# The last matrix product of a fused attention and two-MLP kernel, made of seven block products instead of eight

## The chip, the cores and the metric

The kernel runs on one core of a Trainium2 chip. The metric is the device time of one execution in microseconds (us). The core's engines are TensorE (PE in the views; PEld is its weight load), VectorE (DVE), ScalarE (ACT), GpSimd (POOL) and SyncE (SP), which issues the DMAs. Each takes its instructions in order.

## The reference

```python
attn_out = _attn_ref(q, k, v)                  # 8 batches, 8 heads, 576 tokens, head size 64; k, v pooled by 8
x = attn_out.transpose(0, 2, 1, 3).reshape(B * S, H * D)      # 4608 x 512
x = _moe_ref(x=x, w_in, w_out, g_ln)           # SoLU MLP: softmax, layer norm, 512 -> 1024 -> 512
# second MLP:
a = x @ w1                                     # 4608 x 1024
b = x @ w2
h = a * b @ w3                                 # w3: 1024 x 1024
return (h @ w_out).astype(np.float32)          # w_out: 1024 x 512; called w_out2 in the kernel
```

## The kernel before

The program runs attention and the first MLP interleaved, then the second MLP, in float32. A matrix operand is kept as a rounded half and the rest (helper `split`: ScalarE rounds into the half `hi`, VectorE subtracts into `lo`), and a product is the sum of three matmuls, hi x hi, hi x lo and lo x hi. The second MLP is bilinear before w3, so (a * b) @ w3 @ w_out2 is computed as (a * b) times the 1024 x 512 matrix WF = w3 w_out2.

The 4608 tokens are nine units of 512 (`NB`; eight are one batch's first 512 tokens, the last collects the left-over 64 of each batch). Around the change the program is written out by hand for all five engines, so that each engine's order is that of the code:

1. `ab` makes a * b, transposed, in seven products a pair of blocks, and spills it to DRAM (`pd[j, fc]`: unit j, rows 128 fc to 128 fc + 127 of the 1024, 512 tokens).
2. WF is made in eight blocks of 128 rows. For each, `load_w3` loads 128 rows of w3, `w3_T` transposes them on TensorE (two times four 128 x 128) and splits them out of PSUM, and `wf_rows` multiplies them by the split w_out2 (24 matmuls of 512 columns) and splits the result into an SBUF pair. The transposes of a row block stand ahead of the product of the block before it; two buffers of transposed rows alternate. The text calls these eight blocks rows 0 to 7.
3. The last product: for each unit and each of the eight fc, `product` loads 128 x 512 of `pd`, splits it three steps ahead, and twelve matmuls of 512 columns add to four PSUM banks (`accs`). After the eighth, `evac` scales the four results by a factor of the token (`kap`) and stores them.

PSUM has eight banks, given out in turn by `bank`.

Of the kernel before, what the change touches and what calls it, by code (L numbers as in the profile page):

```python
# [18 lines left out]
def attention_moe_kernel(  # L19
# [1038 lines left out]

    o2, w3raw = [], {}
# [27 lines left out]
    def o2_tiles():  # L1087
        nonlocal STG
        xqs.close()
        STG = ctx.enter_context(tc.tile_pool(name="stage", bufs=1, reuse_waits="tile"))  # L1090
        for f in range(5):
            o2.append(STG.tile([P, 2, 512], F32R, tag=f"o{f}", name=f"o{f}"))

# [3 lines left out]

    STG, o2raw = None, {}

# [11 lines left out]
    def load_w3(m, i):  # L1111
        w3raw[m, i] = staged("w3f", 2 * m + i)

    def w3_pair(m):
        t = TH[(spare, slots[6])[m % 2]].rearrange("p (t f n) -> p t f n", t=2, f=FC)
# [10 lines left out]
    def wf_pair(fc):  # L1126
        t = TH[slots[2 + fc // 2]][:, fc % 2 * 1024 : fc % 2 * 1024 + 1024]
        return t[:, 0:512], t[:, 512:1024]

    def wf_rows(m):  # L1130

        th, tl = w3_pair(m)
# [6 lines left out]
        split(*wf_pair(m), ow)  # L1139

    E = mybir.EngineType
    with tc.manual_schedule(engines={E.PE, E.SP, E.Activation, E.DVE, E.Pool}):
# [22 lines left out]
        for m in range(FC):  # L1165
            for i in range(2):
                if m + 2 < FC:
                    load_w3(m + 2, i)
            for i in range(2):
                if m + 1 < FC:  # L1170
                    w3_T(m + 1, i)
            wf_rows(m)
        products.close()
        sums.close()
        OB = ctx.enter_context(tc.tile_pool(name="out", bufs=1, side="right", reuse_waits="tile"))

        def product(j, fc):
            t, h, l = [
                OB.tile([P, 512], d, tag=n, name=f"{n}{j}_{fc}", bufs=b)
                for n, d, b in (("pt", F32, 8), ("ph", F32R, 4), ("pl", F32R, 4))  # L1180
            ]
            nc.sync.dma_start(t, pd[j, fc])
            nc.scalar.activation(h, t, AF.Copy)  # L1183
            nc.vector.tensor_tensor(l, t, h.bitcast(F32), ALU.subtract)  # L1184
            return h, l

        def evac(j, t, acc):
            ot = OB.tile([P, C], F32, tag="ot", name=f"ot{j}_{t}", bufs=8)
            k = kap[:, 4 * j + t : 4 * j + t + 1]
            if t % 2 == 0:  # L1190
                nc.vector.tensor_scalar(ot, acc, k, None, ALU.mult)
            else:
                nc.scalar.activation(ot, acc, AF.Copy, scale=k)
            if j == B:
# [51 lines left out]
```

## Time and profile before

| | |
|---|---|
| three runs | 1258.39, 1261.03, 1261.51 us, median 1261.03 |
| profiled execution | 1258.51 us, of which the span from first to last instruction is 1256.6 |
| TensorE busy | 1205.6 us (96%), 6794 matmuls |
| VectorE, ScalarE, GpSimd busy | 735.7 (59%), 500.9 (40%), 425.4 us (34%) |
| granted TensorE clock, mean | 0.995 |
| HBM | 99.62 MB read, 48.23 MB written |

Busy time of TensorE is that of matmuls that overlap one another, so 96% says that it hardly pauses. The granted clock is a share of 2.4 GHz; its other level is 0.5, 1.2 GHz. Times in the rows are microseconds from the start of the span, durations us or ns as marked. "Idle before" and the name behind an arrow are the pause of an engine and what ended it.

### The profile page before, as it was taken

Reading aid. Unit: us, or ns where it says so; the run is one execution under the profiler, and the core shown is the slowest. Engines: PE = TensorE matmul, PEld = TensorE weight load, DVE = VectorE, ACT = ScalarE, POOL = GpSimd, SP = SyncE. Lnnn points to the kernel's source line nnn. Section 1 sums busy time; section 2 is a strip of 40 time slices with the busy share of each in tenths; the row PEclk is TensorE's granted clock in tenths of the full one; section 3 lists DMA queues with packets and bytes.
Section 4 is the critical chain, followed back from the end, with each engine's and each line's share of the span. In section 5 each row is a group of like instructions: output and inputs, shape, how many; then the busy total and the mean of one; then the engine's idle time right before and its main releaser. Section 6 shows DMA issues by size and latency. Waiting matters only on the chain. (4 is left out here: it accounts for less than half of the span.)

```text
span 1256.6 us, 18917 instructions
## 1 busy us (share of the span) xinstructions
PE 1205.6 (96%) x6794; PEld 1039.5 (83%) x6794; DVE 735.7 (59%) x1296; ACT 500.9 (40%) x1385; POOL 425.4 (34%) x452
## 2 busy tenths in 40 slices
PE   7868999999999999999898999999999999999998
PEld 5658888899999899999798888888878787888886
DVE  5758776767676767546667656666565622333322
ACT  5544756565656565645522112121121122232222
POOL 3523444344434352200037467494662200000000
PEclk9988999999999999999999999999999999999999
DMA  9561535454445453122341443424412430442533
GB/s 233 112 159 56 143 98 140 106 135 117 124 104 143 109 143 81 59 69 74 114 156 43 134 159 114 141 92 148 159 68 92 142 135 26 144 158 101 188 114 109
DMA packets 148158, 149.11 MB, mean 119 GB/s; under 512 B 81504, under 2 KB 91744, under 8 KB 148064
## 3 DMA queue, kind: packets, MB, share of 16 engines
q1 hardware_dynamic: 148064, 147.90, 39.9%
q8 instruction: 54, 0.88, 0.3%
q14 instruction: 40, 0.33, 0.1%
HBM read 99.62 MB, written 48.23 MB: 118 GB/s over the span
## 5 line engine op out<-in xcount | busy, mean ns | idle before, releaser
L687 PE MATMUL x<-lnh,gwh 128*128 128x256 f32 x576 | 166.1, 288 | 0.0
L688 PE MATMUL x<-lnl,gwh 128*128 128x256 f32 x576 | 163.3, 283 | 0.0
L689 PE MATMUL x<-lnh,gwl 128*128 128x256 f32 x576 | 163.1, 283 | 0.0
L981 ACT ACTIVATE p<-p 128x512 f32<-128x512 f32 (+1 forms) x40 | 22.3, 556 | 268.9 <-PE p L979 227.6
L1184 DVE TENSOR_TENSOR pl<-pt,ph 128x512 fp32r<-128x512 f32 x72 | 49.4, 691 | 128.9 <-ACT ph L1183 112.0
L1212 PE MATMUL acc<-th,ph 128*128 128x512 f32 x288 | 114.0, 396 | 1.2 <-ACT ph L1183 1.2
L1214 PE MATMUL acc<-th,pl 128*128 128x512 f32 x288 | 114.0, 396 | 0.1
L1213 PE MATMUL acc<-th,ph 128*128 128x512 f32 x288 | 113.9, 395 | 0.0
L688 PEld LDWEIGHTS x<-lnl,gwh 128*128 128x128 f32 x576 | 110.3, 191 | 1.3 <-DVE lnl L677 0.4
L687 PEld LDWEIGHTS x<-lnh,gwh 128*128 128x128 f32 x576 | 110.3, 191 | 1.0 <-DVE lnl L677 0.2
L689 PEld LDWEIGHTS x<-lnh,gwl 128*128 128x128 f32 x576 | 110.2, 191 | 0.0
L515 ACT ACTIVATE ea<-sc,mx 128x72 f32<-128x72 f32 x320 | 98.2, 331 | 14.7 <-DVE mx L512 13.7
L630 PE MATMUL h<-winh,xh 128*128 128x512 f32 x288 | 97.6, 420 | 2.9 <-DVE e L645 2.9
L1183 ACT ACTIVATE ph<-pt 128x512 fp32r<-128x512 f32 x72 | 45.2, 632 | 122.2 <-PE acc L1213 86.9
L535 POOL TENSOR_TENSOR pr<-ea,sm 128x512 f32<-128x512 f32 x40 | 43.2, 1080 | 147.4 <-DVE sm L531 69.5
L630 PE MATMUL h<-winl,xh 128*128 128x512 f32 x288 | 89.7, 393 | 0.0
L630 PE MATMUL h<-winh,xl 128*128 128x512 f32 x288 | 89.3, 392 | 0.0
L993 POOL TENSOR_TENSOR a<-a,b 128x512 f32<-128x512 f32 (+1 forms) x40 | 51.8, 1296 | 90.6 <-issue 72.9
L185 POOL TENSOR_TENSOR cvb<-cvb,cvm 128x512 int32<-128x512 int32 x33 | 42.8, 1297 | 98.1 <-DVE cvb L179 62.6
L677 DVE TENSOR_TENSOR lnl<-lt,lnh 128x512 fp32r<-128x512 f32 x72 | 49.2, 687 | 40.6 <-ACT lnh L676 40.0
L515 ACT ACTIVATION_READ_ACCUMULATOR ea<-sc,mx 128x1 f32 x320 | 69.6, 218 | 0.0
L1212 PEld LDWEIGHTS acc<-th,ph 128*128 128x128 f32 x288 | 54.1, 188 | 14.7 <-ACT ph L1183 1.6
(228 smaller groups left out, 3164.2 us busy)
## 6 DMA issues: line engine op xcount, KB each, us to landing
pt<-pd SPq DMA_DIRECT2D x72, 256.0 KB
pd<-a SPq DMA_DIRECT2D x64, 256.0 KB
out_dram<-ot SPq DMA_DIRECT2D x36, 256.0 KB
x2d<-xo SPq DMA_DIRECT2D x35, 256.0 KB
f<-in_moe_w_dram SPq DMA_DIRECT2D x17, 512.0 KB
kv<-in_k_dram SPq DMA_DIRECT2D x32, 256.0 KB
kv<-in_v_dram SPq DMA_DIRECT2D x32, 256.0 KB
f<-in_moe_w_out_dram SPq DMA_DIRECT2D x16, 512.0 KB
```

The source lines that it names most:

```text
L515: nc.scalar.activation(e[0:n, x], half[a][:, h], AF.Exp, bias=mx[0:n, x : x + 1], scale=1.0, accum_out=sm[0:n, x : x + 1],)
L630: nc.tensor.matmul(self.ph[:, a], s_[:, c], w_[:, c, a * 512 : a * 512 + 512], start=first, stop=last)
L677: after(1, lambda: nc.vector.tensor_tensor(lo, src, hi.bitcast(F32), ALU.subtract), first=0)
L687: nc.tensor.matmul(o, gw[0][:, f, ws], self.th[:, f], start=(f == 0), stop=False)
L688: nc.tensor.matmul(o, gw[0][:, f, ws], self.tl[:, f], start=False, stop=False)
L689: nc.tensor.matmul(o, gw[1][:, f, ws], self.th[:, f], start=False, stop=(f == FC - 1))
L993: nc.gpsimd.tensor_tensor(a[:, 0], a[:, 0], b[:, 0], ALU.mult)
L1183: nc.scalar.activation(h, t, AF.Copy)
L1184: nc.vector.tensor_tensor(l, t, h.bitcast(F32), ALU.subtract)
L1212: nc.tensor.matmul(accs[t], ph[:, ts], wh, start=(fc == 0), stop=False)
L1213: nc.tensor.matmul(accs[t], ph[:, ts], wl, start=False, stop=False)
L1214: nc.tensor.matmul(accs[t], pl[:, ts], wh, start=False, stop=(fc == FC - 1))
```

## The change

The last product is written as a 2 x 2 block product in seven multiplications. For unit j the four blocks of the left matrix are x11, x21 (first 512 of the 1024, first and second 256 tokens), x12, x22; those of WF are its upper and lower half by left and right 256 columns. GpSimd forms four sums of left blocks (`Last.sum`), and each of the seven factors of 4 x 128 x 256 is split (`Last.split`, one instruction of 128 x 1024 on ScalarE and one on VectorE). The seven combinations of WF are formed while WF is made: its row blocks come in pairs, one of the upper and one of the lower half (`HALVES`), `upper` keeps the first in SBUF, and `lower` makes differences and splits six combinations. `Last.product` multiplies (24 matmuls of 256 columns), `Last.use` adds the products (VectorE out of PSUM), scales the finished rows in SBUF (ScalarE) and stores them. The factors of unit j + 1 are split during unit j, in the order of its products; the loads of unit j + 2 are issued at the start of unit j. Unit 0's own come in `early`, its last three at the start of its products. The odd buffer of transposed rows moves to another tile.

```diff
+    HALVES = (0, 4, 1, 5, 2, 6, 3, 7)
...
     def load_w3(m, i):
-        w3raw[m, i] = staged("w3f", 2 * m + i)
+        w3raw[m, i] = staged("w3f", 2 * HALVES[m] + i)
     def w3_pair(m):
-        t = TH[(spare, slots[6])[m % 2]].rearrange("p (t f n) -> p t f n", t=2, f=FC)
+        t = TH[(spare, slots[5])[m % 2]].rearrange("p (t f n) -> p t f n", t=2, f=FC)
         return t[:, 0], t[:, 1]
...
-    def wf_pair(fc):
-        t = TH[slots[2 + fc // 2]][:, fc % 2 * 1024 : fc % 2 * 1024 + 1024]
-        return t[:, 0:512], t[:, 512:1024]
-    def wf_rows(m):
-        th, tl = w3_pair(m)
+    def wf_rows(n):
+        m = HALVES[n]
+        th, tl = w3_pair(n)
         ow = bank(f"ow{m}")
         for f in range(FC):
             oh, ol = o2[f][:, 0], o2[f][:, 1]
             nc.tensor.matmul(ow, th[:, f], oh, start=(f == 0), stop=False)
             nc.tensor.matmul(ow, th[:, f], ol, start=False, stop=False)
             nc.tensor.matmul(ow, tl[:, f], oh, start=False, stop=(f == FC - 1))
-        split(*wf_pair(m), ow)
+        return ow
+    def combined(k, c):
+        if k < 4:
+            return [t[:, k, c * U : c * U + U] for t in wc]
+        t = TH[slots[k - 2]].rearrange("p (t c n) -> p t c n", t=2, c=4)
+        return t[:, 0, c], t[:, 1, c]
+    def small(name, bufs=1):
+        return RB.tile([P, U], F32, tag=name, name=name, bufs=bufs)
+    def upper(c, ow):
+        w1_ = RB.tile([P, 2, U], F32, tag="wf", name="wf", bufs=2)
+        nc.scalar.activation(w1_, ow.rearrange("p (h n) -> p h n", h=2), AF.Copy)
+        split(*combined(0, c), w1_[:, 0])
+        t1 = small("t1")
+        nc.gpsimd.tensor_tensor(t1, w1_[:, 1], w1_[:, 0], ALU.subtract)
+        return w1_[:, 1], t1
+    def lower(c, ow, w12, t1):
+        tt = nc.vector.tensor_tensor
+        w21, w22 = ow[:, 0:U], ow[:, U : 2 * U]
+        t2, t3, t4 = small("t2"), small("t3"), small("t4")
+        split(*combined(3, c), w21)
+        tt(t2, w22, t1, ALU.subtract)
+        split(*combined(1, c), t2)
+        split(*combined(2, c), t1)
+        tt(t3, w22, w12, ALU.subtract)
+        split(*combined(4, c), t3)
+        tt(t4, w21, t2, ALU.subtract)
+        split(*combined(5, c), t4)
+        split(*combined(6, c), w22)
+    FACTORS = ("x11", "s2", "s1", "x12", "s3", "x22", "s4")
+    free = list(range(10))
+    class Last:
+        def __init__(self, j):
+            self.j, self.x, self.place = j, {}, {}
+            self.order = range(7) if j else (0, 3, 1, 2, 4, 5, 6)
+        def load(self, k):
+            t = RB.tile([P, 4, 512], F32, tag="raw", name=f"raw{self.j}_{k}", bufs=4)
+            nc.sync.dma_start(t, pd[self.j, 4 * k : 4 * k + 4].rearrange("f p n -> p f n"))
+            for i in range(2):
+                self.x[f"x{i + 1}{k + 1}"] = t[:, :, i * U : i * U + U]
+        def sum(self, name):
+            x = self.x
+            a, b, op = dict(
+                s1=("x21", "x22", ALU.add),
+                s2=("s1", "x11", ALU.subtract),
+                s3=("x11", "x21", ALU.subtract),
+                s4=("x12", "s2", ALU.subtract),
+            )[name]
+            x[name] = RB.tile([P, 4, U], F32, tag="s", name=f"{name}_{self.j}", bufs=4)
+            nc.gpsimd.tensor_tensor(x[name], x[a], x[b], op)
+        def split(self, k):
+            n = self.place[k] = free.pop(0)
+            t = BK[n].rearrange("p (t c n) -> p t c n", t=2, c=4)
+            split(t[:, 0], t[:, 1], self.x[FACTORS[k]])
+            self.x[k] = t[:, 0], t[:, 1]
+        def product(self, n):
+            k = self.order[n]
+            h, l = self.x[k]
+            o = bank(f"o{k}_{self.j}").rearrange("p (t n) -> p t n", t=2)
+            for t in range(2):
+                ts = slice(t * P, t * P + P)
+                for c in range(4):
+                    wh, wl = combined(k, c)
+                    nc.tensor.matmul(o[:, t], h[:, c, ts], wh, start=(c == 0), stop=False)
+                    nc.tensor.matmul(o[:, t], h[:, c, ts], wl, start=False, stop=False)
+                    nc.tensor.matmul(o[:, t], l[:, c, ts], wh, start=False, stop=(c == 3))
+            free.append(self.place[k])
+            self.use(k, o)
+        def scale(self, t, src, dst, i):
+            n = 4 * self.j + 2 * i + t
+            nc.scalar.activation(dst, src, AF.Copy, scale=kap[:, n : n + 1])
+        def tile(self, name):
+            return OT.tile([P, 2, U], F32, tag=name, name=f"{name}_{self.j}")
+        def store(self, i, t=None):
+            if self.j == B:
+                to = out.rearrange("(b s) c -> s b c", s=S)[512:S, 4 * i + 2 * t : 4 * i + 2 * t + 2, :]
+                nc.sync.dma_start(to, self.rows[i][:, t])
+            else:
+                r0 = S * self.j + 2 * P * i
+                nc.sync.dma_start(out[r0 : r0 + 2 * P].rearrange("(t p) c -> p t c", p=P), self.rows[i])
+        def use(self, k, o):
+            tt = nc.vector.tensor_tensor
+            lo, hi = slice(0, U), slice(U, 2 * U)
+            if k == 0:
+                self.p1 = self.tile("p1")
+                self.rows = [
+                    OT.tile([P, 2, C], F32, tag="rows", name=f"rows{self.j}_{i}", bufs=4) for i in range(2)
+                ]
+                nc.scalar.activation(self.p1, o, AF.Copy)
+            elif k == 1:
+                self.u2 = self.tile("u2")
+                tt(self.u2, self.p1, o, ALU.add)
+            elif k == 2:
+                self.u4 = self.tile("u4")
+                tt(self.u4, self.u2, o, ALU.add)
+            elif k == 3:
+                r = self.rows[0]
+                tt(r[:, :, lo], self.p1, o, ALU.add)
+            elif k == 4:
+                self.u3 = self.tile("u3")
+                tt(self.u3, self.u2, o, ALU.add)
+                tt(self.rows[1][:, :, hi], self.u4, o, ALU.add)
+            else:
+                i, x, cs = (1, self.u3, lo) if k == 5 else (0, self.u4, hi)
+                r = self.rows[i]
+                if self.j < B:
+                    tt(r[:, :, cs], x, o, ALU.add)
+                for t in range(2):
+                    if self.j == B:
+                        tt(r[:, t, cs], x[:, t], o[:, t], ALU.add)
+                    self.scale(t, r[:, t], r[:, t], i)
+                    if self.j == B:
+                        self.store(i, t)
+                if self.j < B:
+                    self.store(i)
...
         products.close()
         sums.close()
-        OB = ctx.enter_context(tc.tile_pool(name="out", bufs=1, side="right", reuse_waits="tile"))
...
+        RB = ctx.enter_context(tc.tile_pool(name="last", bufs=1, side="right", reuse_waits="tile"))
+        BK = [RB.tile([P, 2048], F32R, tag=f"bk{i}", name=f"bk{i}") for i in range(6)]
+        BK += [TH[i] for i in (spare, slots[0], slots[1], slots[5])]
+        wc = weight_pair(wp, "w16", [P, 4, F], "wc")
+        last = [Last(j) for j in range(NB)]
+        z = last[0]
+        early = {
+            1: [(z.load, 0)],
+            2: [(z.load, 1)],
+            3: [(z.split, 0)],
+            4: [(z.sum, "s1"), (z.sum, "s2"), (z.split, 3), (last[1].load, 0)],
+            5: [(z.sum, "s3"), (z.sum, "s4"), (z.split, 1), (last[1].load, 1)],
+            7: [(z.split, 2), (last[1].sum, "s1")],
+        }
+        for n in range(FC):
+            for i in range(2):
+                if n + 2 < FC:
+                    load_w3(n + 2, i)
+            for i in range(2):
+                if n + 1 < FC:
+                    w3_T(n + 1, i)
+            ow = wf_rows(n)
+            if n % 2 == 0:
+                w12, t1 = upper(n // 2, ow)
             else:
+                lower(n // 2, ow, w12, t1)
+            for fn, *args in early.get(n, ()):
+                fn(*args)
+        stg.close()
+        OT = ctx.enter_context(tc.tile_pool(name="out", bufs=1, reuse_waits="tile"))
+        for j, un in enumerate(last):
+            n1_, n2_ = [last[i] if i < NB else None for i in (j + 1, j + 2)]
+            for n in range(7):
+                if n == 0 and n2_:
+                    n2_.load(0)
+                    n2_.load(1)
+                if n1_ and n in (0, 2, 4):
+                    n1_.sum(("s2", "s3", "s4")[n // 2])
+                if n == 6 and n2_:
+                    n2_.sum("s1")
+                if un is z and n < 3:
+                    z.split(4 + n)
+                if n1_:
+                    n1_.split(n1_.order[n])
+                un.product(n)
```

ScalarE between row 5 and row 7 of WF. In the names, `pw6` are the transposed rows of row 6, `ow` are products of rows (numbered by their place in WF), and `th0`, `th6`, `th7` the buffers of transposed rows; the text calls the splits of `pw7` row 7's. Before:

```order
L100 ACTIVATE th0_7258<-pw6_0_10429 128x512
L100 ACTIVATE th0_7258<-pw6_1_10436 128x512
L100 ACTIVATE th5_7263<-ow5_10443 128x512
L100 ACTIVATE th7_7307<-pw7_0_10470 128x512
L100 ACTIVATE th7_7307<-pw7_1_10477 128x512
```

After (`t1` to `t4` are differences of WF's blocks, `wch` holds the rounded combinations 0 to 3, `th3` to `th5` those of 4 to 6, `bk2` a split factor, `s2_0` a sum of unit 0):

```order
L100 ACTIVATE th0_7258<-pw6_0_10501 128x512
L100 ACTIVATE th0_7258<-pw6_1_10508 128x512
L100 ACTIVATE wch_10212<-ow6_10515 128x256
L100 ACTIVATE wch_10212<-t2_10540 128x256
L100 ACTIVATE wch_10212<-t1_10487 128x256
L100 ACTIVATE th3_7261<-t3_10541 128x256
L100 ACTIVATE th4_7262<-t4_10542 128x256
L100 ACTIVATE th5_7263<-ow6_10515 128x256
L100 ACTIVATE bk2_10208<-s2_0_10491 128x1024
L100 ACTIVATE th6_7264<-pw7_0_10566 128x512
L100 ACTIVATE th6_7264<-pw7_1_10573 128x512
```

Between the splits of row 6 and those of row 7 there was one rounding; now there are six, each but the first and last of a difference made by another engine, and one of 1024 columns.

VectorE in the last product, unit 3 before (`pl` is the rest of a split, `ot` a scaled result):

```order
L1184 TENSOR_TENSOR pl3_3_11044<-pt3_3_11042,ph3_3_11043 128x512
L1184 TENSOR_TENSOR pl3_4_11066<-pt3_4_11064,ph3_4_11065 128x512
L1184 TENSOR_TENSOR pl3_5_11084<-pt3_5_11082,ph3_5_11083 128x512
L1184 TENSOR_TENSOR pl3_6_11102<-pt3_6_11100,ph3_6_11101 128x512
L1184 TENSOR_TENSOR pl3_7_11120<-pt3_7_11118,ph3_7_11119 128x512
L1184 TENSOR_TENSOR pl4_0_11138<-pt4_0_11136,ph4_0_11137 128x512
L1184 TENSOR_TENSOR pl4_1_11156<-pt4_1_11154,ph4_1_11155 128x512
L1184 TENSOR_TENSOR pl4_2_11174<-pt4_2_11172,ph4_2_11173 128x512
L1191 TENSOR_SCALAR ot3_0_11181<-acc3_0_11048,kap_78 128x512
L1191 TENSOR_SCALAR ot3_2_11193<-acc3_2_11050,kap_78 128x512
```

VectorE during unit 2 after (`o1_2` to `o6_2` are unit 2's products, `bk` and `th` on the left split factors of unit 3; the factors 0 and 1 stand just ahead):

```order
L1245 TENSOR_TENSOR u2_2_11174<-p1_2_11143,o1_2_11149 128x512
L101 TENSOR_TENSOR bk3_10209<-s1_3_11077,bk3_10209 128x1024
L1248 TENSOR_TENSOR u4_2_11205<-u2_2_11174,o2_2_11180 128x512
L101 TENSOR_TENSOR bk4_10210<-raw3_1_10891,bk4_10210 128x1024
L1251 TENSOR_TENSOR rows2_0_11144<-p1_2_11143,o3_2_11209 128x2x256
L101 TENSOR_TENSOR th0_7258<-s3_3_11176,th0_7258 128x1024
L1254 TENSOR_TENSOR u3_2_11264<-u2_2_11174,o4_2_11239 128x512
L1255 TENSOR_TENSOR rows2_1_11145<-u4_2_11205,o4_2_11239 128x2x256
L101 TENSOR_TENSOR th2_7260<-raw3_1_10891,th2_7260 128x1024
L1260 TENSOR_TENSOR rows2_1_11145<-u3_2_11264,o5_2_11269 128x2x256
L101 TENSOR_TENSOR bk5_10211<-s4_3_11235,bk5_10211 128x1024
L1260 TENSOR_TENSOR rows2_0_11144<-u4_2_11205,o6_2_11302 128x2x256
```

Eight subtractions and two scalings have become seven subtractions of double width and seven additions that alternate with them.

ScalarE during unit 3 before (`ph` is the rounded half):

```order
L1193 ACTIVATE ot2_1_11027<-acc2_1_10889,kap_78 128x512
L1193 ACTIVATE ot2_3_11039<-acc2_3_10891,kap_78 128x512
L1183 ACTIVATE ph3_3_11043<-pt3_3_11042 128x512
L1183 ACTIVATE ph3_4_11065<-pt3_4_11064 128x512
L1183 ACTIVATE ph3_5_11083<-pt3_5_11082 128x512
L1183 ACTIVATE ph3_6_11101<-pt3_6_11100 128x512
L1183 ACTIVATE ph3_7_11119<-pt3_7_11118 128x512
```

ScalarE during unit 2 after, with the factors of unit 3:

```order
L100 ACTIVATE bk1_10207<-raw3_0_10889 128x1024
L1242 ACTIVATE p1_2_11143<-o0_2_11118 128x512
L100 ACTIVATE bk2_10208<-s2_3_11114 128x1024
L100 ACTIVATE bk3_10209<-s1_3_11077 128x1024
L100 ACTIVATE bk4_10210<-raw3_1_10891 128x1024
L100 ACTIVATE th0_7258<-s3_3_11176 128x1024
L100 ACTIVATE th2_7260<-raw3_1_10891 128x1024
L1221 ACTIVATE rows2_1_11145<-rows2_1_11145,kap_78 128x512 x2
L100 ACTIVATE bk5_10211<-s4_3_11235 128x1024
L1221 ACTIVATE rows2_0_11144<-rows2_0_11144,kap_78 128x512 x2
```

The scalings of finished rows now stand between the roundings of the last factors, and each pair waits for an addition.

## Rows read from the trace of the kernel before

**Rows 1.** Windows: stretch; busy us of each engine (instructions); clock; DMA share, GB/s.

```profile
997.40:1048.80 51.40, 50.13 (x243) 40.87 (x241) 13.99 (x22) 11.23 (x21) 2.33 (x2) 1.00 0.34 113
1048.80:1050.20 1.40, 0.22 (x1) 0.00 (x0) 0.52 (x1) 1.15 (x3) 0.00 (x0) 1.00 0.00 0
1050.20:1252.30 202.10, 202.01 (x864) 162.01 (x864) 62.06 (x91) 56.23 (x88) 0.00 (x0) 1.00 0.36 125
1252.30:1256.60 4.30, 0.12 (x1) 0.00 (x0) 0.21 (x1) 0.69 (x1) 0.00 (x0) 1.00 0.66 244
```

**Rows 2.** Chain that ended last, two pieces in w3 w_out2: start, us, what.

```profile
1011.36 0.87 PE pw L1121 x8
1017.73 0.87 PE pw L1121 x8
```

**Rows 3.** TensorE's timeline, two stretches: start, us, line, operation, out<-in.

```profile
608.77 0.28 PE L687 MATMUL x<-lnh,gwh 128*128 128x256 f32 x1
...
611.89 0.28 PE L689 MATMUL x<-lnh,gwl 128*128 128x256 f32 x1
...
654.94 0.28 PE L977 MATMUL p<-th,s2h 128*128 128x256 f32 x1
...
656.94 0.28 PE L979 MATMUL p<-th,w1l 128*128 128x256 f32 x1
```

**Rows 4.** Groups of instructions: line, form, count; busy us, mean ns; idle before.

```profile
L1212 PEld LDWEIGHTS acc<-th,ph 128*128 128x128 f32 x288 | 54.1, 188 | 14.7 <-ACT ph L1183 1.6
L1183 ACT ACTIVATE ph<-pt 128x512 fp32r<-128x512 f32 x72 | 45.2, 632 | 122.2 <-PE acc L1213 86.9 <-DMA pt<-pd 33.9 <-DVE pl L1184 0.7
L100 ACT ACTIVATE th<-pw 128x512 fp32r<-128x512 f32 x16 | 8.9, 598 | 5.5 <-PE pw L1121 5.4
L983 DVE TENSOR_TENSOR u<-p,p 128x256 f32<-128x256 f32 x8 | 3.3, 416 | 3.2 <-PE p L979 3.2
L981 ACT ACTIVATE p<-p 128x256 f32<-128x256 f32 x8 | 3.1, 383 | 29.1 <-PE p L979 26.2 <-DVE a L987 2.9
```

**Rows 5.** Instructions of three lines of 1024 columns: ns min/median/max, starts.

```profile
L926 DVE TENSOR_TENSOR th<-xq,th x16: 1212/1330/3196, 661.8 to 918.5; 128x1024 fp32r<-128x1024 f32 x16
...
L862 POOL TENSOR_TENSOR xq<-xq,xq x16: 2389/2404/3383, 656.0 to 910.7; 128x1024 f32<-128x1024 f32 x16
...
L919 ACT ACTIVATE th<-xq x28: 1048/1060/1066, 660.4 to 915.8; 128x1024 fp32r<-128x1024 f32 x28
```

**Rows 6.** Timelines of VectorE and GpSimd at three places.

```profile
661.82 3.20 DVE L926 TENSOR_TENSOR th<-xq,th 128x1024 fp32r<-128x1024 f32 x1
...
661.54 2.40 POOL L862 TENSOR_TENSOR xq<-xq,xq 128x1024 f32<-128x1024 f32 x1
663.89 1.72 POOL L997 TENSOR_TENSOR a<-a,b 128x256 f32<-128x256 f32 x1
...
667.95 0.73 POOL L993 TENSOR_TENSOR a<-a,b 128x256 f32<-128x256 f32 x1
668.65 3.38 POOL L862 TENSOR_TENSOR xq<-xq,xq 128x1024 f32<-128x1024 f32 x1
...
668.13 1.64 DVE L926 TENSOR_TENSOR th<-xq,th 128x1024 fp32r<-128x1024 f32 x1
...
906.15 0.69 DVE L989 TENSOR_TENSOR b<-u,p 128x512 f32<-128x512 f32 x1 [2.14 <-POOL a L997]
...
906.08 2.40 POOL L862 TENSOR_TENSOR xq<-xq,xq 128x1024 f32<-128x1024 f32 x1
```

**Rows 7.** TensorE after a long wait: its timeline, and a window as in rows 1.

```profile
98.65 1.11 PE L560 MATMUL pt<-ident,pr 128*128 128x128 f32 x4 [3.84 <-POOL pr L535]
...
98.00:103.00 5.00, 4.35 (x21) 4.35 (x22) 4.13 (x9) 3.14 (x18) 2.55 (x4) 0.50 0.31 107
```

**Rows 8.** A window as in rows 1, in which the DMA engines are full.

```profile
1075.00:1080.00 5.00, 5.00 (x23) 4.04 (x22) 1.81 (x3) 1.90 (x3) 0.00 (x0) 1.00 1.02 342
```

**Rows 9.** ScalarE's timeline at the end.

```profile
1252.46 0.69 ACT L1193 ACTIVATE ot<-acc,kap 128x512 f32<-128x512 f32 x1 [0.71 <-PE acc L1214]
```

More of the change, by code (lines that the diff above doesn't have):

```diff
@@ L1089, in o2_tiles @@
         xqs.close()
-        STG = ctx.enter_context(tc.tile_pool(name="stage", bufs=1, reuse_waits="tile"))
+        STG = stg.enter_context(tc.tile_pool(name="stage", bufs=1, reuse_waits="tile"))
         for f in range(5):
@@ L1096, in late_o2 @@
             o2.append(TH[slots[n]][:, 1024 * h : 1024 * h + 1024].rearrange("p (t n) -> p t n", t=2))
-    STG, o2raw = None, {}
+    STG, o2raw, stg = None, {}, ExitStack()
     def staged(name, i):
@@ L1164, in attention_moe_kernel @@
                     slots, spare = [spare] + slots[:6], slots[6]
[L1165 to L1172, printed above, removed]
         products.close()
         sums.close()
-        OB = ctx.enter_context(tc.tile_pool(name="out", bufs=1, side="right", reuse_waits="tile"))
[L1177 to L1191, printed above, removed]
-            else:
-                nc.scalar.activation(ot, acc, AF.Copy, scale=k)
-            if j == B:
-                to = out.rearrange("(b s) c -> s b c", s=S)[512:S, 2 * t : 2 * t + 2, :]
-            else:
-                to = out[S * j + P * t : S * j + P * t + P, :]
-            nc.sync.dma_start(to, ot)
@@ L1200, in attention_moe_kernel @@
-        order = [(j, fc) for j in range(NB) for fc in range(FC)]
-        AHEAD = 3
-        ready = {o: product(*o) for o in order[:AHEAD]}
-        for n, (j, fc) in enumerate(order):
-            if n + AHEAD < len(order):
-                ready[order[n + AHEAD]] = product(*order[n + AHEAD])
-            if fc == 0:
-                accs = [bank(f"acc{j}_{t}") for t in range(4)]
-            ph, pl = ready.pop((j, fc))
-            wh, wl = wf_pair(fc)
-            for t in range(4):
-                ts = slice(t * P, t * P + P)
-                nc.tensor.matmul(accs[t], ph[:, ts], wh, start=(fc == 0), stop=False)
-                nc.tensor.matmul(accs[t], ph[:, ts], wl, start=False, stop=False)
-                nc.tensor.matmul(accs[t], pl[:, ts], wh, start=False, stop=(fc == FC - 1))
-                if fc == FC - 1:
-                    evac(j, t, accs[t])
+        RB = ctx.enter_context(tc.tile_pool(name="last", bufs=1, side="right", reuse_waits="tile"))
```

## The prediction

> **What bounds the kernel now.** I read first the windows over the end of the program, then the chain of waits, then the rows of the engines that the change gives work to. The windows [rows 1] show TensorE busy for 50.1 of the 51.4 us in which w3 w_out2 is made, then a gap of 1.4 us, then 864 matmuls of 512 columns in 202.1 us without a pause (233.9 ns each), then 4.3 us in which the last rows are scaled and stored. In the same 202 us VectorE is busy for 62 us, ScalarE for 56 and GpSimd for none. The chain of waits [rows 2] runs through TensorE's own instructions from row to row of w3 w_out2, one row each 6.4 us (0.87 us of transposes and some 5.5 us of matmuls). So TensorE sets the time here, and fewer matmul columns are worth their full price as long as the other three engines keep up with the seven-product scheme. That is the question of this change.
>
> **Matmuls taken out.** A block of 512 tokens had 96 matmuls of 512 columns and gets 7 x 24 = 168 of 256. Matmuls of 256 columns with a new weight for each follow one another at 120.0 ns in the first MLP (26 steps in 3.12 us) and at 117.6 ns in the single-block product (17 steps in 2.00 us) [rows 3]. With 119 ns a block takes 20.0 us (19.8 to 20.2) instead of 22.5, and nine take 180 instead of 202.1. The gap of 1.4 us before them goes too: the first factor is split two rows earlier, and the first product waits for no row but the last upper one. From the end E of the last row to the last matmul, 203.5 us would become 180.
>
> **What VectorE, ScalarE and GpSimd get.** Per block: seven splits of 128x1024 (ScalarE 1.06 us for the rounded half, VectorE 1.2 for the rest) and four GpSimd sums of 128x1024 (2.4) [rows 5]; seven VectorE additions out of PSUM (0.69 for 512 columns [rows 6]); one ScalarE copy out of PSUM (0.6) and four scalings of 512 columns in SBUF (0.63) [rows 4]. Busy time alone is 13.2 us on VectorE, 10.5 on ScalarE, 9.6 on GpSimd, all under 20.
>
> But two of them exclude each other. In [rows 6] a VectorE subtraction of two SBUF operands starts at 661.82 while a GpSimd sum holds from 661.54 to 663.94, and takes 3.20 us in place of 1.2: it ends 1.1 us after the sum. The GpSimd product behind it takes 1.72 us in place of 0.73. At 668.65 it is the sum that waits for the subtraction (3.38). An addition with a PSUM operand at 906.15 keeps its 0.69 under a sum. So subtractions of splits (8.4 us a block) and sums (9.6 us) run one at a time, 18.0 of the 20 us, and VectorE, which works in order, stands still while a sum passes.
>
> The period of a block, if VectorE is the one that is late (order excerpt of VectorE), counted from the last addition of a block: two scalings 1.26, rounding 1.06, subtraction 1.2 make 3.5; the next rounding comes behind the copy (0.6), so the second subtraction ends at 5.2; then addition and subtraction alternate up to the addition of product 5 at 14.1; its two scalings and the rounding behind them take 2.3, subtraction and addition 1.9: 18.3 us without a sum. Twice in it VectorE waits for ScalarE (2.3 us each, behind scalings), and a sum that falls there is hidden. One that falls elsewhere costs 2.4 less the additions beside it: 1.7, or 1.0 at the double addition. The sum s1 of the block after next waits for that block's loads, which SyncE issues behind the stores of the last block: two loads of 1 MB and a store of 0.5 MB at 342 GB/s [rows 8] are 7.7 us, with the way to landing about 11 us into the period. s1 to s4 follow there. Two hidden and two not gives 21.0; one hidden 22.7. I take the middle, 21.8, because s1 arrives near the second ScalarE wait and s4 near the first, and s2 and s3 then stand in the way of a subtraction. That is 1.8 more than TensorE's 20.0 and 0.7 less than the 22.5 of before: most of the gain of the matmuls is taken back.
>
> **The first block.** Its last three factors are split after E, and three things stand ahead: the last lower row's relay between ScalarE and VectorE (six roundings of 0.38 and nine operations of 0.42 [rows 4], about 5.4 us), the split of s1 (to 7.3) and of s3 (to 8.5). Then sums of the next block alternate with subtractions: sum to 10.9, subtraction 12.1, sum 14.5, x22's subtraction 15.7; product 5 wants it at 14.5 and waits 1.2. Sum, subtraction, addition, and s4's subtraction ends at 21.2 where product 6 wants it at 18.6: 2.6 more. TensorE ends block 0 at E + 23.8. VectorE has five subtractions (6.0), six additions (4.1), one ScalarE wait (2.3) and some 4.4 us of sums left, and ends its part at E + 38. From there six periods P pass until it starts on the last block's factors, 3.5 us later TensorE can start that block, and 20.0 later it is through: E + 61.5 + 6P. Were TensorE alone to decide, it would be 23.8 + 160 = E + 183.8. P = 21.8 gives E + 192.3; 21.0 gives 187.5, 22.7 gives 197.7. Until TensorE has used up the lead that it starts with (VectorE is a block behind by then) it doesn't wait; from the third or fourth block it does.
>
> **A new wait in w3 w_out2.** The rows' matmuls are the same. But ScalarE and VectorE now do the combinations and splits between the rows' operands (order excerpt of ScalarE). After row 5 ends, TensorE needs the transposed row 7 split 6.5 us later (0.87 + 5.6). Ahead of that split stand the lower row's relay (5.4 us, four of its subtractions on SBUF alone) and s2's split; and GpSimd's four sums of block 0 run from 1.8 to 13.3 us after row 4's end, so up to 6.8 us into this stretch. Two of the relay's subtractions wait 1.9 and 1.6 us for sums; the relay ends at 8.7, the roundings of s2 and of row 7's first half at 9.9, its subtraction at 11.3. TensorE waits 3.5 and then 0.8 us: 4.4, or 5.2 if the waiting sum goes first each time that both want in, which no row shows; I take 4.7. After a wait of 3.84 us the granted clock was 0.50 from 98 to 103 us [rows 7], which would add 2.5; a wait of 3.5 is shorter than that one, so I put it at nothing and keep 2.5 for the range. In row 5 the same relay meets no sums and has 0.87 us more: 0 to 0.3, left out.
>
> **The end.** Before, one scaling of 0.69 lies between last matmul and last store [rows 9]. Now two additions of 256 columns and two scalings do, partly side by side: 0.42 + 0.63 + 0.63 = 1.7: +1.0. Loads and stores are as many bytes as before, and 4 MB of loads that start during w3 w_out2 share its 113 GB/s [rows 1] with room up to 342: nothing.
>
> **Sum.** 192.3 - 203.5 = -11.2; +4.7; +1.0: -5.5 us on the profiled execution's 1258.5, so 1253.0. The median of the runs shown is 2.5 above that execution; I add 1 and forecast 1254.
>
> **A rule against it.** The Trainium skill says in "TensorE: Matmul & The Clock Gate", section "The mechanism", that a weight load overlaps running matmuls only when it goes to another row group; here each load fills the array. By its section "LDWEIGHTS (loading the stationary operand)", 128/1.2 = 107 ns a load, this is an estimate of 214 ns for each of 1512 matmuls, 323 us. The trace disagrees: 233.9 ns for 512 columns and 119 for 256 leave about 4 ns that don't shrink with the columns.
>
> **Rivals.**
> - Everything hides (0.22). For it: busy times are under 20 us, and banks and buffers let VectorE lag by six products. If sums fall only into VectorE's waits, P is 20 or less: 183.8 - 203.5 + 5.7 = -14.0, 1245.5 in the forecast's terms; without exclusion (180, and a wait of 1 us in row 7) -21.5, 1238. Against it: [rows 6].
> - The block period is over before's (0.18). Three exposed sums (P = 22.7) with the clock's 2.5 give -5.8 + 4.7 + 2.5 + 1.0 = +2.4, 1262; the kernel is slower than before from P = 22.7 on, by over 0.3% from 23.4, or 22.9 with the clock. For it: relays between four engines have small delays that I don't count, a tenth at each of a dozen handovers. Against it: TensorE's lead covers the first blocks.
> - Each matmul pays its weight load (0.02): with the load's 188 ns [rows 4] on top of 119, 1512 x 307 ns = 464 us, 262 more. Against it: [rows 3].
>
> **How the numbers follow.** The forecast has 0.52, its own range 1248 to 1262 (P 21.0 with 4.4, to P 22.7 with 5.2 and the clock); 0.06 is left for what I don't see. The range 1241 to 1264 leaves out most of the unhindered case and what is over P = 23. 0.3% is 3.8 us, about what runs of this kernel can tell from no change. Faster: 0.36 of the forecast's 0.52, all 0.22, 0.02 = 0.60. Same: 0.14 + 0.08 + 0.02 = 0.24. Slower: 0.02 + 0.10 + 0.02 + 0.02 = 0.16.
>
> **What would show it.** Right: TensorE pauses of 3 to 5 us before the last row, 1 to 3 in the first block, and from the third or fourth block about 1.8 us a block, put down to VectorE; VectorE's 1024-wide subtractions with a mean well over 1.2; block starts 20 us apart first and 21 to 23 later. Wrong: TensorE at 119 ns without pauses (then sums hide), or blocks more than 23 us apart.

## The result and the profile after

The changed kernel takes 1246.19 us (median of four runs, 1243.80 to 1248.27) against 1260.05 for the kernel before beside it (1258.39 to 1261.51): a ratio of 0.989 with a 95% interval of 0.9865 to 0.9914, 13.9 us less. The profiled execution took 1248.27, its span 1246.5. The forecast was 1254 with a range of 1241 to 1264: the sign and the range hold, but the time lies below the 1248 to 1262 of the forecast's own case, and the gain is two and a half times the 5.5 us that the sum gave.

The windows of the changed kernel over the end of the program answer to [rows 1]: w3 w_out2, the last product, and what follows the last matmul (columns as there).

```profile
1002.90:1060.90 58.00, 53.45 (x243) 42.72 (x242) 33.34 (x49) 20.39 (x43) 18.10 (x11) 0.94 0.46 154
1060.90:1240.90 180.00, 178.92 (x1513) 178.46 (x1512) 138.87 (x132) 85.75 (x109) 86.58 (x31) 1.00 0.35 124
1240.90:1246.50 5.60, 0.24 (x3) 0.04 (x1) 0.75 (x2) 1.95 (x4) 0.00 (x0) 0.71 0.48 187
```

The last product went from 1.4 + 202.1 to 180.0 us (-23.5), w3 w_out2 from 51.4 to 58.0 (+6.6), the end from 4.3 to 5.6 (+1.3): together -15.6 us. The execution as a whole gained 10.2 (1258.51 to 1248.27), since row 0 begins 5.5 us later in it (1002.9 instead of 997.4), behind stages that the change doesn't touch; a low clock around 680 us, which the profile of before doesn't have, is a part of that. In the ten profiles with the new last product row 0 begins between 998.8 and 1003.5, so most of the 5.5 us is within what executions of these stages differ by.

In those 180 us VectorE is busy for 139, which was 62. So the question is how near it came to holding TensorE up. TensorE's waits from 990 us on (engine, line, whom it waited for; us in total, times, longest):

```profile
PE ow L1134 <- ACT th L100: 3.0, 1, 3.0
PE o L1215 <- DVE th L101: 1.1, 2, 0.6
PE ow L1136 <- DVE th L101: 0.9, 2, 0.5
PE pw L1122 <- DMA stg<-w3f: 0.6, 1, 0.6
```

In nine blocks TensorE waits twice for VectorE, 0.6 and 0.5 us: once in the first block, once at the start of the last. The costly wait is the new one before row 7 of w3 w_out2 (the first line and a part of the third). TensorE there:

```profile
1048.27 0.39 PE L1136 MATMUL ow<-th,th 128*128 128x512 f32 x1
1051.69 0.50 PE L1134 MATMUL ow<-o,th 128*128 128x512 f32 x1 [3.03 <-ACT th L100]
...
1053.06 0.80 PE L1136 MATMUL ow<-o,th 128*128 128x512 f32 x1 [0.52 <-DVE th L101]
...
1057.92 0.63 PE L1135 MATMUL ow<-o,th 128*128 128x512 f32 x1
1058.35 0.63 PE L1136 MATMUL ow<-o,th 128*128 128x512 f32 x1
1058.78 0.49 PE L1134 MATMUL ow<-th,th 128*128 128x512 f32 x1
1059.10 0.40 PE L1135 MATMUL ow<-th,th 128*128 128x512 f32 x1
```

Matmuls of 512 columns start 0.23 us apart at the full clock; the pause before 1051.69 is 3.42 us, so 3.2 are lost, and 0.7 more before 1053.06. Then they start 0.43 us apart until 1058.78: the granted clock fell to its lower level behind the wait, which costs another 3.0 us. What made row 7 late can be read on VectorE, GpSimd and ScalarE, one fence each:

```profile
1039.27 3.41 DVE L101 TENSOR_TENSOR bk<-raw,bk 128x1024 fp32r<-128x1024 f32 x1
1042.60 1.28 DVE L101 TENSOR_TENSOR th<-pw,th 128x512 fp32r<-128x512 f32 x2
...
1045.03 2.88 DVE L101 TENSOR_TENSOR wcl<-t,wch 128x256 fp32r<-128x256 f32 x2 [0.49 <-ACT wch L100]
...
1052.33 1.28 DVE L101 TENSOR_TENSOR th<-pw,th 128x512 fp32r<-128x512 f32 x2
```

```profile
1039.14 2.45 POOL L1197 TENSOR_TENSOR s<-s,raw 128x1024 f32<-128x1024 f32 x1
1041.56 3.37 POOL L1197 TENSOR_TENSOR s<-raw 128x1024 f32<-128x1024 f32 x1
1044.88 2.41 POOL L1197 TENSOR_TENSOR s<-raw,s 128x1024 f32<-128x1024 f32 x1
```

```profile
1049.84 0.36 ACT L100 ACTIVATE th<-ow 128x256 fp32r<-128x256 f32 x1
1050.10 1.05 ACT L100 ACTIVATE bk<-s 128x1024 fp32r<-128x1024 f32 x1
1051.05 1.07 ACT L100 ACTIVATE th<-pw 128x512 fp32r<-128x512 f32 x2
```

A subtraction for unit 0 starts just behind a sum and takes 3.41 us for 1.2; the lower row's relay starts behind it, and its own subtraction at 1045.03 stands behind the next sum (2.88 for two of 0.4). ScalarE's last rounding of the relay ends at 1050.2, then it rounds s2, and only then row 7's first half. That rounding starts at 1051.05, 9.6 us after row 5's end at 1041.4; the forecast had it at 9.3.

### The profile page after: what moved, and what is told of

It is laid out like the page before. It is cut to its first block, busy times and chain, and to the rows that moved or that the text cites. A ratio compares the mean times of both kernels' runs of the same rounds, so it can differ in the third digit from the quotient of the medians.

```text
span 1246.5 us, 20344 instructions
## 1 busy us (share of the span) xinstructions
PE 1189.1 (95%) x7442; PEld 1060.6 (85%) x7442; DVE 831.4 (67%) x1366; ACT 539.0 (43%) x1427; POOL 528.5 (42%) x492
## 5 line engine op out<-in xcount | busy, mean ns | idle before, releaser
L630 PEld LDWEIGHTS h<-winl,xh 128*128 128x128 f32 x288 | 54.2, 188 | 12.4
L630 PEld LDWEIGHTS h<-winh,xl 128*128 128x128 f32 x288 | 54.1, 188 | 12.3
L1221 ACT ACTIVATE rows<-rows,kap 128x512 f32<-128x512 f32 x36 | 24.1, 716 | 90.2 <-DVE rows L1260 86.5
L639 ACT ACTIVATE e<-h,ST 128x1024 f32<-128x1024 f32 x36 | 40.1, 1114 | 52.9 <-DVE ST L638 52.8
L676 ACT ACTIVATE lnh<-lt 128x512 fp32r<-128x512 f32 x72 | 43.2, 605 | 39.1 <-PE lt L673 38.9
L978 PE MATMUL p<-th,w1h 128*128 128x512 f32 (+1 forms) x160 | 59.5, 372 | 0.5 <-POOL th L926 0.5
```

What stands on the lines that cost most here:

```text
L630: nc.tensor.matmul(self.ph[:, a], s_[:, c], w_[:, c, a * 512 : a * 512 + 512], start=first, stop=last)
L676: nc.scalar.activation(hi, src, AF.Copy)
L978: nc.tensor.matmul(o, wh[:, c, fsl], tl[:, c], start=False, stop=False)
```

## The experiments

The table has the nine runs beside the changed kernel: median us, ratio to the kernel before with its 95% interval, then from the profile the length of w3 w_out2 (first matmul of row 0 to first of the last product), that of the last product, and what TensorE waited in it for VectorE.

| run | us | ratio | WF | product | waits |
|---|---|---|---|---|---|
| the change | 1246.19 | 0.989 (0.9865 to 0.9914) | 58.0 | 180.0 | 1.1 |
| e1_relay_late | 1237.88 | 0.9824 (0.9809 to 0.9838) | 49.8 | 180.4 | 1.7 |
| e2_one_more_addition | 1249.08 | 0.9903 (0.9883 to 0.9924) | 56.6 | 184.0 | 3.8 |
| e3_no_sums | 1236.56 | 0.9805 (0.9792 to 0.9818) | 51.4 | 178.2 | 0 |
| e4_one_more_sum | 1255.93 | 0.996 (0.9947 to 0.9974) | 57.5 | 190.5 | 7.1 |
| e5_late_and_ahead | 1237.08 | 0.9813 (0.9796 to 0.983) | 49.6 | 180.0 | 1.4 |
| e7_ahead_and_addition | 1244.30 | 0.9865 (0.985 to 0.9881) | 57.7 | 179.1 | 0.6 |
| e8_eighth_product | 1268.13 | 1.0052 (1.0037 to 1.0066) | 57.2 | 204.5 | 0.6 |
| e9_best | 1236.71 | 0.9807 (0.979 to 0.9824) | 49.7 | 180.0 | 1.4 |
| e10_first_block_early | 1242.43 | 0.9843 (0.9829 to 0.9857) | 49.9 | 184.3 | 4.4 |

Theory A: GpSimd's sums and VectorE's subtractions exclude each other, that and ScalarE's handovers give VectorE a period of its own of 20.2 us, and it reaches the end of the last product together with TensorE, with nothing to spare. Theory B: VectorE has room, and its period is only TensorE's.

**Row 7's order.**

```diff
             for i in range(2):
                 if n + 1 < FC:
                     w3_T(n + 1, i)
+            if n in (2, 4, 6):
+                lower(n // 2 - 1, ow, w12, t1)
             ow = wf_rows(n)
             if n % 2 == 0:
                 w12, t1 = upper(n // 2, ow)
-            else:
-                lower(n // 2, ow, w12, t1)
+            if n == 7:
+                lower(3, ow, w12, t1)
...
-            5: [(z.sum, "s3"), (z.sum, "s4"), (z.split, 1), (last[1].load, 1)],
+            5: [(z.sum, "s3"), (z.sum, "s4"), (last[1].load, 1)],
+            6: [(z.split, 1)],
```

> The six combinations of a lower row (and unit 0's split of s2) are emitted behind the splits of the next row's transposes, on ScalarE and VectorE alike; nothing else moves. Theory A (the wait of 3.9 us before row 7 is only an order of instructions, the half clock behind it follows from it, and VectorE and TensorE reach the end of the last product at about the same time): the wait and the half clock vanish, row 7 follows row 6 at full clock, w3 w_out2 takes 51 to 52 us instead of 58, and 5 to 7 us of the time go; what is missing to 7 shows as new waits of TensorE for VectorE's subtractions in the last product, since the moved work now runs later against TensorE. Theory B (VectorE has room to spare in the last product, its pace is only that of TensorE): the full 7 us, and TensorE waits 1.1 us in the last product as before.

The windows of this run, in the same order:

```profile
1003.40:1053.20 49.80, 49.49 (x243) 41.08 (x242) 29.06 (x49) 20.30 (x43) 15.85 (x10) 1.00 0.52 180
1053.20:1233.70 180.50, 178.82 (x1513) 178.37 (x1512) 139.74 (x133) 85.76 (x109) 88.83 (x32) 1.00 0.35 123
```

The wait is gone, and with it the half clock (1.00 where it was 0.94): w3 w_out2 is 8.2 us shorter, and so is the time, 8.3. At 49.8 us it is even shorter than the 51 to 52 that I expected and the 51.4 of before. The order alone takes the wait away. Between A and B this run says little: TensorE's waits in the last product grew from 1.1 to 1.7 us, as A has it, but that is small.

**What is left on VectorE.** The addition of u2 is done twice.

```diff
                 tt(self.u2, self.p1, o, ALU.add)
+                tt(self.u2, self.p1, o, ALU.add)
```

> The addition that makes u2 is done twice in each of the nine blocks: 0.68 us more of VectorE a block, beside operands that it has anyway. Theory A (VectorE is level with TensorE in the last product, its period of 20.2 us is its own): seven periods get 0.68 longer, TensorE waits for VectorE's subtractions in the last blocks, the time is 4 to 5 us longer. Theory B (room to spare): no change, within 1 us.

TensorE's waits in the last product:

```profile
PE o L1215 <- DVE th L101: 3.8, 5, 1.2
```

The last product is 4.0 us longer for an operation of 0.68 on an engine that was busy for 139 of 180 us. From the first matmul of the last product to the end of the program it is 5.8 us (191.3 for 185.5). A had 4 to 5 us; B, no change, is excluded for this stage. The time of the whole doesn't decide: the medians are 2.9 us apart and the intervals overlap. In this profile w3 w_out2 was 1.4 us shorter, as the low clock behind row 7's wait was shorter, and row 0 began 3.7 us earlier.

**The sums left out.**

```diff
-            x[name] = RB.tile([P, 4, U], F32, tag="s", name=f"{name}_{self.j}", bufs=4)
-            nc.gpsimd.tensor_tensor(x[name], x[a], x[b], op)
+            x[name] = x[dict(s1="x21", s2="x11", s3="x11", s4="x12")[name]]
```

> GpSimd's four sums of each unit are left out (the split takes one of the two operands as it is), so the result isn't the product. Theory A (VectorE's subtractions and the sums exclude each other, and that lengthens VectorE's period and row 7's wait): all VectorE subtractions of 1024 columns take 1.2 us, its period comes to 18.3 us, the 1.4 us that TensorE waits in the last product go, row 7 waits 0 to 1.5 us instead of 3.9 and keeps the full clock: 6 to 8 us less. Rival on row 7 (the handovers between ScalarE and VectorE alone make it late): the wait stays over 3 us and only 1 to 2 us go. Theory B gives the last product the same 180 us either way.

VectorE's groups in the last product of this run (count, busy us, mean ns, idle before):

```profile
L101 DVE TENSOR_TENSOR bk<-raw,bk 128x1024 fp32r<-128x1024 f32 x36 | 43.8, 1221 | 22.5 <-ACT bk L100 22.5
L101 DVE TENSOR_TENSOR th<-raw,th 128x1024 fp32r<-128x1024 f32 x24 | 29.2, 1222 | 14.8 <-ACT th L100 14.8
...
L1253 DVE TENSOR_TENSOR u<-u,o 128x512 f32<-128x512 f32 x9 | 6.2, 686 | 8.3 <-PE o L1214 8.3
```

And the same subtractions in the last product of the changed kernel:

```profile
L101 DVE TENSOR_TENSOR bk<-s,bk 128x1024 fp32r<-128x1024 f32 x21 | 33.5, 1600 | 14.8 <-ACT bk L100 14.8
...
L101 DVE TENSOR_TENSOR bk<-raw,bk 128x1024 fp32r<-128x1024 f32 x15 | 29.3, 1956 | 7.1 <-ACT bk L100 7.1
...
L101 DVE TENSOR_TENSOR th<-s,th 128x1024 fp32r<-128x1024 f32 x14 | 20.5, 1468 | 5.3 <-ACT th L100 5.3
...
L101 DVE TENSOR_TENSOR th<-raw,th 128x1024 fp32r<-128x1024 f32 x10 | 17.9, 1789 | 9.4 <-ACT th L100 9.4
```

Without sums every subtraction takes 1.22 us; with them the same 60 take 101.2 us, 1.69 in the mean. VectorE now waits for TensorE's products (the last row of the first fence), which from 1095 to 1215 us it never does in the changed kernel: here it has room. TensorE's 1512 matmuls run without a wait in 178.2 us, 117.9 ns each, so A's tie cost it only 1.8 us. In w3 w_out2 one wait of 0.6 us is left before row 7's third matmul and the clock stays full: the sums, not the handovers alone, made row 7 late. VectorE's first period from last addition to last addition is 17.3 us, from the third on it is TensorE's 19.8.

**One more sum.**

```diff
-            nc.gpsimd.tensor_tensor(x[name], x[a], x[b], op)
+            for i in range(2 if name == "s1" and self.j > 1 else 1):
+                nc.gpsimd.tensor_tensor(x[name], x[a], x[b], op)
```

> GpSimd's sum s1 is done twice for units 2 to 8: 2.4 us more of GpSimd a block, seven times. Theory A: sums and subtractions, which exclude each other, are 20.4 us a block instead of 18.0, the period of VectorE grows by 0.5 to 1.7 us, and as VectorE is level with TensorE the time is 3 to 10 us longer. Theory B (GpSimd has 10 us of idle time in a block, VectorE room to spare): no change, within 1 us.

TensorE's waits in the last product of this run:

```profile
PE o L1216 <- DVE th L101: 4.2, 5, 2.2
PE o L1216 <- DVE bk L101: 2.9, 2, 1.8
```

The last product takes 10.5 us more and the time is 9.7 longer, at A's upper end: 1.5 us for each of seven sums of 2.4 on an engine that is busy for 87 of 180 us. A part of the 10.5 isn't waits: the clock is 0.98 over the product, low twice behind such a wait.

**Where VectorE's period comes from.** In the changed kernel it waits twice a block for a rounding that stands behind two scalings on ScalarE. Here the rounding goes first (`split` calls `round`, which does nothing a second time): in e5_late_and_ahead on top of e1's order, in e7_ahead_and_addition in the order of the change, with e2's second addition.

```diff
                 if n1_:
                     n1_.split(n1_.order[n])
+                    if n < 6:
+                        n1_.round(n1_.order[n + 1])
+                    elif n2_:
+                        n2_.round(0)
                 un.product(n)
```

> The order of e1_relay_late, and in the last product each factor's rounding on ScalarE one product earlier, ahead of the scalings that VectorE's next subtraction waited behind (2.35 us twice a block). Theory A with C (these two waits are what makes VectorE's period 20 us and more): VectorE gets ahead, the 1.7 us that TensorE waits in the last product with e1 go, the product takes 178.2 us, the time is 1 to 2 us under that of e1, some 1236. Theory A with D (the exclusion decides: sums that passed during those waits now stand in the way of subtractions, 4 x 1.7 us on top of 13.2 us busy): VectorE's period stays near 20, and the time is that of e1 within 1 us.

> The changed kernel with each factor's rounding one product earlier, and with the addition that makes u2 done twice (as in e2): row 7 keeps its wait. C: the additional 0.68 us a block find room in the 4.7 us of ScalarE waits that are gone: the last product takes 178 to 180 us instead of the 184 of e2, the time is 4 to 6 us under that of e2. D: VectorE is as late as in e2, 183 to 185 us.

VectorE's waits from 1095 to 1215 us, in the changed kernel and then in e5_late_and_ahead:

```profile
DVE bk L101 <- ACT bk L100: 16.7, 8, 2.4
DVE th L101 <- ACT th L100: 12.4, 8, 2.4
```

```profile
DVE bk L1202 <- ACT bk L1209: 4.0, 2, 3.4
```

Of 29.1 us of waits 4.0 are left, and in e7_ahead_and_addition none. There the doubled addition, which cost 4.0 us in e2, costs nothing: the last product takes 179.1 us, 4.9 less than in e2, and the time is 4.8 less. So C holds for the period: VectorE's last additions are 18.7 us apart in e5 and 19.2 in e7, for 20.2 in the changed kernel. But D is true in part: what the 49 subtractions of seven blocks take beyond 1.22 us adds up to 38.7 us in e5 where it was 19.7. Sums that had passed in the waits now stand in the way, 2.7 us a block, and take back two thirds of the 4.2 us of waits that each block lost. The time of e5 is that of e1 (their intervals overlap): TensorE had waits of 1.7 us to lose in the last product, and lost 0.3, since the wait of the first block (1.4 us) stayed.

**The eighth product.**

```diff
-                for c in range(4):
+                cs = [0, 1, 2, 3] * (2 if k == 6 else 1)
+                for i, c in enumerate(cs):
```

> The seventh product of each block is accumulated twice over (24 matmuls more a block, 216 in all, and a result that isn't the product); all else as in the changed kernel. If the gain of the change is the eighth product that it saves, 216 x 118 ns = 25.5 us come back, less the 1.4 us that TensorE waited for VectorE, which now has 22.9 us a block: the last product takes 203.7 us, the time is about 1270. If part of the gain lies in the other form (256 columns, no gap, fewer loads), the last product stays under 200.

With 192 matmuls of 256 columns a block the last product takes 204.5 us, 1.0 more than the 203.5 of before, and the time is 0.52% over that of before. So the gain is the eighth product, not the other form; without it the other costs of the change, 6.6 and 1.3 us, are left as a loss (7.1 us between the medians).

**The end.** On top of e5_late_and_ahead, the last unit's seventh product goes to two banks.

```diff
             for t in range(2):
+                if last:
+                    o = bank(f"o{k}_{self.j}_{t}").rearrange("p (t n) -> p t n", t=2)
...
+                if last:
+                    self.use(k, o, (t,))
```

> As e5_late_and_ahead, and the last unit's seventh product goes to two banks, so that its first 128 tokens are added, scaled and stored while TensorE works on the other 128. From the last matmul to the end of the span 0.6 to 1.0 us less than the 5.6 us of the changed kernel; with e5 some 1235. If the stores' way to landing decides alone, the end stays as it is.

```profile
1228.50:1233.40 4.90, 0.24 (x3) 0.04 (x1) 0.42 (x1) 0.78 (x2) 0.00 (x0) 0.75 0.55 211
```

The end is 4.9 us for 5.6, as expected. This is the lowest ratio of the kernels that compute the whole, 0.9807 of before; against e1 (0.9824) the difference is within the intervals, and only the profile shows where it is from.

**An attempt at the first block that failed**, on top of e9_best.

```diff
-            6: [(z.split, 1)],
-            7: [(z.split, 2), (last[1].sum, "s1")],
+            6: [(z.split, 1), (z.split, 2), (z.split, 4), (z.split, 5), (last[1].sum, "s1")],
...
-                if un is z and n < 3:
-                    z.split(4 + n)
+                if un is z and n == 0:
+                    z.split(6)
```

> As e9_best, and unit 0's splits of s1, s3 and x22 stand in row 6 of w3 w_out2 instead of behind the last row, with unit 1's sum s1 behind them. The one wait that TensorE has left in the last product of e9_best (1.4 us in block 0, for the split of x22, whose subtraction stands behind a sum of GpSimd) goes: the last product takes 178.3 us instead of 179.9, and the time is 1.5 us under that of e9_best. If the more splits in row 6 make row 7's or the last row's own work late, that wait comes back elsewhere, 1 to 3 us, and the time is that of e9_best or longer.

VectorE of this run around the last row, and TensorE's wait in block 0:

```profile
1049.09 5.71 DVE L1202 TENSOR_TENSOR bk<-s,bk 128x1024 fp32r<-128x1024 f32 x3 [0.34 <-ACT bk L1209]
1054.73 3.35 DVE L1202 TENSOR_TENSOR bk<-raw,bk 128x1024 fp32r<-128x1024 f32 x1
1058.01 0.41 DVE L101 TENSOR_TENSOR wcl<-ow,wch 128x256 fp32r<-128x256 f32 x1
```

```profile
1058.47 0.58 PE L1224 MATMUL o<-wcl,bk 128*128 128x256 f32 x1 [4.36 <-DVE wcl L101]
```

The second case came true, with a longer wait than the 1 to 3 us expected. The last row's first combination (`wcl<-ow`), which the second product of block 0 needs, now stands behind four subtractions, two of them held by sums (9 us for 4.9), and TensorE waits 4.4 us for it. In the orders tried VectorE is late around the end of w3 w_out2: what was moved forward there pushed something else back.

## Why the prediction was right in sign and too small in size

**TensorE's price** was right within 1%: 180 us from 168 matmuls a block at 119 ns, and 178.2 were measured where nothing waits (e3, 117.9 ns each); the eighth product costs what was taken off for it (e8).

**The parts of the mechanism on VectorE** were right too. Sums and subtractions exclude each other (e3), a further sum costs 1.5 us (e4; 1.7 or 1.0 was in the working), the ScalarE waits of 2.35 us come twice a block (2.3 in the working), and VectorE's own path sets the end (e2). What failed is what they add up to. VectorE was to be late enough to take 12.3 us back (E + 192.3 for 180), "most of the gain of the matmuls"; it took 1.8 (180.0 for the 178.2 of e3). The terms of E + 192.3:

| term | predicted | measured |
|---|---|---|
| E to VectorE's last addition of block 0 | 38 | 33.1 |
| six periods | 6 x 21.8 = 130.8 | 121.4, 20.2 each |
| from there to TensorE's start of the last block | 3.5 | 5.8 |
| the last block | 20.0 | 19.6 |
| sum | 192.3 | 179.9 |

The measured terms go from start to start; the addition of block 0 ends at E + 33.8. The step that failed first is the first block. The working has two sums of unit 1 ahead of x22's subtraction and a third between it and s4's. In the run unit 1's s1 had passed before E, the two are s2 and s3, and the third isn't there. GpSimd and VectorE of the changed kernel, one fence each:

```profile
1053.37 2.38 POOL L1197 TENSOR_TENSOR s<-raw,raw 128x1024 f32<-128x1024 f32 x1
```

```profile
1072.49 3.43 DVE L101 TENSOR_TENSOR th<-raw,th 128x1024 fp32r<-128x1024 f32 x1
...
1077.58 2.35 DVE L101 TENSOR_TENSOR th<-s,th 128x1024 fp32r<-128x1024 f32 x2
```

E is 1060.96. x22's subtraction ends at E + 15 (15.7 was forecast), s4's at E + 17.8 instead of 21.2, and TensorE waits 0.6 us in the block, not 3.8. This is read from the traces; no run puts the sum back.

The second is the period. VectorE from the last addition of one block to that of the next:

```profile
1135.08 0.67 DVE L1260 TENSOR_TENSOR rows<-u,o 128x512 f32<-128x512 f32 x1
1138.11 1.22 DVE L101 TENSOR_TENSOR th<-raw,th 128x1024 fp32r<-128x1024 f32 x1 [2.35 <-ACT th L100]
1139.54 1.23 DVE L101 TENSOR_TENSOR th<-s,th 128x1024 fp32r<-128x1024 f32 x1 [0.21 <-ACT th L100]
1140.68 0.68 DVE L1245 TENSOR_TENSOR u<-p,o 128x512 f32<-128x512 f32 x1
1141.28 1.22 DVE L101 TENSOR_TENSOR bk<-s,bk 128x1024 fp32r<-128x1024 f32 x1
...
1147.08 3.33 DVE L101 TENSOR_TENSOR bk<-raw,bk 128x1024 fp32r<-128x1024 f32 x1
1150.33 0.67 DVE L1260 TENSOR_TENSOR rows<-u,o 128x512 f32<-128x512 f32 x1
1153.36 2.77 DVE L101 TENSOR_TENSOR bk<-s,bk 128x1024 fp32r<-128x1024 f32 x1 [2.36 <-ACT bk L100]
1156.05 0.67 DVE L1260 TENSOR_TENSOR rows<-u,o 128x512 f32<-128x512 f32 x1
```

It is what the working describes, in its better case: two sums pass in the ScalarE waits or beside additions, two reach into subtractions (3.33 and 2.77), 21.0 us. The six periods are 19.0, 22.0, 21.0, 19.0, 21.1 and 19.3. Sums take 2.9 of the mean of 20.2 (3.5 were forecast), and the path without them is 17.3, not 18.3 (e3's first period): an addition is shown as 0.68 but the next instruction starts 0.60 later, and 1.14 behind a subtraction of 1.22, and I had added durations. Seven pairs make 1.0 us of that.

The third row of the table went the other way, 5.8 for 3.5: a sum from 1217.72 to 1220.14 reaches into the subtraction of the last block's first factor, which is 1.5 of the 2.3 us; the rest is the addition at the row's start.

```profile
1218.46 2.77 DVE L101 TENSOR_TENSOR th<-raw,th 128x1024 fp32r<-128x1024 f32 x1 [2.36 <-ACT th L100]
```

Together the first block and the period put VectorE's end within 2 us of TensorE's own (178.2 without sums). So the pauses of 1.8 us a block that the prediction named as its sign aren't there. The time is near that of the rival in which everything hides (1245.5), but not by its mechanism, which had the sums fall into VectorE's waits alone: here they lengthen subtractions to 1.69 us in the mean, and 0.68 us more on VectorE cost 4.0 in the product (e2). That its number fits is luck in part: it had the last product 3.8 us too long and the rest 2.2 too short.

**The weight load of each matmul**, the third rival, was nowhere to be seen. Of the changed kernel's groups in the last product, the loads of one line:

```profile
L1213 PEld LDWEIGHTS o<-wch,bk 128*128 128x128 f32 x176 | 33.2, 188 | 0.0
```

The loads are shown with 188 to 192 ns, and the matmuls start 118 to 119 ns apart.

**The wait in row 7** was forecast as 4.7 us and is 3.9, from the causes named: relay, s2's split and sums (e1 takes it away by order, e3 by leaving out the sums). What failed is "I put it at nothing" for the clock: 3.0 us. **The end** was +1.0 and is +1.3.

## What to carry to other kernels

An engine that is busy for 77% can have no slack at all, if it works in order and its instructions wait for two other engines; the test is to add one small instruction a period and see whether the stage grows by most of it. When durations from a trace are added up to a period, take the distances between starts, and place each helper's first instructions on the clock before counting how many stand in the way. And when work is put between the stages of a pipeline, what feeds the next matmuls goes first in the order of every engine: here that alone was worth 8.3 us, where the change had brought 13.9.

## What the runs showed of the hardware

**The granted clock behind a wait.** A pause of 3.4 us before row 7 (3.0 to 3.1 in the view of waits, as the lengths that follow are) was followed by the lower clock in all five profiles that have it (the change, e2, e4, e7, e8), one of 4.4 us in e10 too, and where the pause was gone the clock stayed at 1.00 (e1, e3, e5, e9). In w3 w_out2 the low stretch was once half as long as in the other four (e2, with w3 w_out2 1.4 us shorter for it). But the length of the pause alone doesn't decide. Around 675 us, in a stage that is the same in all kernels, TensorE waits 2.5 to 3.5 us for VectorE; the clock stayed full behind 3.50 us in the kernel before and fell behind 2.64 in e1. Around 600 us, also behind a wait for VectorE, it fell in three of the eleven profiles (1.88 us in e1, 1.95 in e10, 2.04 in e8) and stayed full in the others, behind 2.00 us in e5 too. I had taken a wait shorter than the 3.84 of [rows 7] as harmless, and no row said so.

**Who goes next.** When a sum and a subtraction both wait for each other's end, they alternate: in the fence of row 7 the subtraction from 1039.27 ends 1.1 us after the sum of 1039.14 to 1041.59, and the sum of 1041.56 ends 2.3 us after that. No subtraction of 1024 columns in any run took more than 3.45 us, so none let two sums pass. The Trainium skill, "SBUF — State Buffer", section "SBUF: two separate sides", says that an operation of VectorE with two SBUF inputs and a GpSimd operation that reads SBUF exclude each other on a shared pair of ports, and that whichever starts first keeps it for its whole instruction. The trace agrees: in the changed kernel 3.43 us for 1.22 behind a sum (1072.49), and 0.68 for an addition with a PSUM operand under one (1079.85, the sum ends at 1082.18).
